# Roots of the last token group taken in one piece, and the first chunk's second layer run high weights first, in a fused attention and two-MoE kernel

## The chip, the cores and the metric

The kernel runs on one core of a Trainium2 chip. The metric is the device time of one execution in microseconds (us). TensorE is called PE here, VectorE DVE, ScalarE ACT, GpSimd POOL and SyncE, which issues most of the DMAs, SP. PE's weight loads are listed on their own as PEld.

## The reference, cut to what matters

Three layers stand one behind the other. Linear attention gives 4608 tokens of 512 values, normed by a root mean square per head of 64. A first mixture of experts routes each token to the expert with the largest logit. A second one, which this change does not touch, assigns 576 tokens to each of 8 experts.

```python
def _attn_ref(q, k, v, g_norm):
    kv = np.einsum('bhsd,bhse->bhde', k, v)
    out = np.einsum('bhsd,bhde->bhse', q, kv)
    rms = np.sqrt(np.mean(out * out, axis=-1, keepdims=True) + 1e-06)
    return (out / rms * g_norm).astype(np.float32)

def _moe_ref(x, expert_emb, tau, w1, w2):
    ...
    logits = xn @ en.T / tau
    expert_idx = np.argmax(logits, axis=1)
    ...
    for e in range(E):
        mask = expert_idx == e
        h = np.maximum(x[mask] @ w1[e], 0.0)
        out[mask] = gate_w[mask, None] * (h @ w2[e])
```

## The kernel before, in words

**Groups and steps.** The tokens come in four groups (gi 0 to 3) of nine tiles. Each group takes ten steps i. A step transposes a piece of q two steps ahead (`qa`: PE into `tp`, ACT copies to `qT`) and multiplies an earlier piece by the kv product (`qb`: PE into a bank `mm`; ACT copies the result to `xo`, squares it to `sq` and copies the logits to `lp`). DVE sums the squares of the step before to `s`. The last two steps are the short tail (`xt`).

**The group's end.** `group_end(gi)` takes roots of the sums (`rsqrt`: a square root on ACT, then four DVE operations on `yy`, `ww`, `r`), scales the logits, reduces them over the heads to `lg`, finds the expert (`mx`, `w`, `ix`, one-hot `P`) and stores the rows to `xbuf`. `slots()` then multiplies `P` by triangular and full matrices on PE (`trm`, `ones`), scans the counts (`bs`, `ue`, `run`), builds one-hots (`ohb`, `oha`) and has PE add them to a table of slots (`table`, `tabi`). It is a generator: `pump()` or `next(ge)` takes it one stage further, so its engine work lies between the steps in the order written. For the last group `part` splits the roots into columns of tiles 0 and 1, of 2 and 3, and of 4, and `LASTP` says at which steps the stages are taken.

**First expert, first chunk.** Slots of expert 0 filled by the first three groups (320 columns, tiles 0 to 2) are gathered early from `xbuf` (`xg`, and `kvx` for the third), scaled by their roots (`normed`), and transposed (`xtile`) to high and low parts `xh`, `xl` at the steps that `XT0` names. `first0` runs both expert layers on that chunk: 192 matmuls of 320 columns, three products for each weight (high weight by high and low data, low weight by high data). `stream` hands them out in portions (`PEW`, in us), between which the last group's end is emitted; `ROWS` places the transposes of the remaining tiles 3 to 5 near the end. The chunk's banks `mm` are two: a layer-1 bank is free again when DVE has written `hl` from it. Tiles 3 to 5 are gathered once the last group's `table` is done, and chunk 1 (288 columns) begins with them.

**Weights.** A piece is 128 x 1024 numbers (512 KB), loaded to one of three buffers `wraw` by SP; ACT casts it to `whi`, and DVE takes the rest to `wlo`, which frees the buffer. Pieces 0 to 3 are layer 1 of expert 0, 4 to 7 layer 2. `LSUB` holds DVE parts that are put off until after the gather.

**Aside.** `w2g_ops` is a list of small DVE products (`rc`, 128 of them) that prepare second-router weights for experts 6 and 7. `ASIDE` says how many are emitted at five places of each of the experts 1 to 5; some are left over for expert 6, which takes one after each of four layer-1 pieces, and `run_gen(wg)` takes what remains.

Of the kernel before, what the change touches and what calls it, by code (L numbers as in the profile page):

```python
# [7 lines left out]
F32 = mybir.dt.float32  # L8
# [30 lines left out]

SURE = 6  # L40

ASIDE = (1, 5, 6, 6, 3)

EARLY = 0

PEW = ((1, 2.0), (1, 4.2), (1, 2.0), (2, 3.3))

EVAC = (
# [7 lines left out]

LOADS = {19: 1, 21: 2, 23: 3, 27: 4, 30: 5, 31: 6}

LASTP = (4, 5, 6, 8, 9)

NSQ = 4

NYR = 4

XT0 = (4, 5, 5)

ROWS = (2.6, 1.3, 0.2)

# [12 lines left out]
def fused_kernel(ctx, tc, q, k, v, g_norm, emb, tau, w1, w2, wgate, v1, v2, out):  # L81
# [146 lines left out]
    def run_gen(g):  # L228
        for _ in g:
            pass  # L230
# [155 lines left out]
    def group_end(gi):  # L386
# [31 lines left out]
        def part(a, b):  # L418

            c = slice(16 * a, min(16 * b, TG * H))  # L420
            V.tensor_scalar(uu[:, c], s1[:, c], 1.0 / D, 1e-6, op0=OP.mult, op1=OP.add)
            if last:
                yield
            yield from rsqrt(r[:, c], uu[:, c], yy[:, c], ww[:, c])
            V.tensor_tensor(lp[:, c], lp[:, c], r[:, c, None].to_broadcast([128, c.stop - c.start, E]), op=OP.mult)

            f, of = lp.rearrange("p c n -> p (c n)"), lg.rearrange("p c n -> p (c n)")
            m = min(b, 4)
            if a < m:
                V.tensor_reduce(of[:, 16 * a:16 * m].rearrange("p (a x) -> p a x", a=m - a),  # L430
                                f[:, 128 * a:128 * m].rearrange("p (a h x) -> p a x h", a=m - a, h=H), axis=AX.X, op=OP.add)
            if b == 5:
                V.tensor_reduce(of[:, 64:], f[:, 512:].rearrange("p (h x) -> p x h", h=H), axis=AX.X, op=OP.add)
            for u_ in range(a, b):
                m = 2 if u_ < 4 else 1
                x = G["x", u_]
                nc.gpsimd.tensor_copy(x[:, :, HD:HD + E], lg[:, 2 * u_:2 * u_ + m])
                if u_ < 4:
                    nc.gpsimd.tensor_copy(x[:, :, HD + E:], r[:, 16 * u_:16 * u_ + 16].rearrange("p (h r) -> p r h", r=2))
                else:  # L440
                    nc.gpsimd.tensor_copy(x[:, 0, HD + E:].rearrange("p (g h s) -> p g s h", g=2, h=2),
                                          r[:, 64:72].rearrange("p (g s h) -> p g s h", g=2, s=2))

        if last:

            p0, p1, p2 = part(0, 2), part(2, 4), part(4, 5)
            next(p0)
            yield
            next(p0)
            yield  # L450
            run_gen(p0)
            yield
            next(p1)
            yield
            next(p1)
            yield
            next(p2)
            next(p2)
            run_gen(p1)
            yield  # L460
            run_gen(p2)
            for u_ in range(5):
                store(u_)
        else:
            yield from part(0, 5)
            yield
        w = t8("w")
        mx = mk(gp, [128, TG], F32, "mx", bufs=2)
# [94 lines left out]
    def wload(upto, q=nc.sync):  # L563
        while WS["load"] < min(upto, len(WQ)):
            key, t, off, pat = WQ[WS["load"]]
            raw = mk(wpA, [128, 1024], F32, "wraw", bufs=3)
            q.dma_start(raw.rearrange("p (a c) -> p a c", c=pat[-1][1]), src(t, off, pat))
            RAW[key] = raw
            WS["load"] += 1
# [166 lines left out]
    def layer1(m, e, f, c):  # L736
        run_gen(layer1_g(m, e, f, c))

    def layer1_g(m, e, f, c):

        N = WID[m, e][c]
        keep = (m, e) == (0, E - 1)
        if f == 0 and not keep:
            k = SLOT[m, e][c]
            HT[m, e, c] = [mk(mp, [128, KF, COLS[k]], F32R, f"h{p}{k}") for p in "hl"]
        whi, wlo = (w.rearrange("p (a c) -> p a c", a=KD) for w in WT[m, e, 0, f])
        xh, xl = XT[m, e, c]
        ps = mk(psum, [128, 2, 512], F32, "mm")
        for t in range(2):
            o = ps[:, t, :N]  # L750
            for kd in range(KD):
                a, b = whi[:, kd, t * 128:(t + 1) * 128], wlo[:, kd, t * 128:(t + 1) * 128]
                nc.tensor.matmul(o, a, xh[:, kd, :N], start=(kd == 0), stop=False)  # L753
                nc.tensor.matmul(o, a, xl[:, kd, :N], start=False, stop=False)  # L754
                nc.tensor.matmul(o, b, xh[:, kd, :N], start=False, stop=(kd == KD - 1))  # L755
                yield 3 * N / 2400
# [20 lines left out]
    def layer2_g(e, c, dp, mid=None):  # L777

        N = WID[0, e][c]
        if dp == 0:  # L780
            k = SLOT[0, e][c]
            YT[e, c] = mk(mp, [128, KD, COLS[k]], F32, f"yT{k}")
        hh, hl = HT[0, e, c]
        apart = (e, c, dp) == (E - 1, 1, 1)
        ps = mk(psum, [128, 2, 512], F32, "mm")
        order = [(t, kf) for t in range(2) for kf in range(KF)]
        if (e, c, dp) == (0, 0, 0):
            order.sort(key=lambda x: x[1] // (KF // 2))
        for t, kf in order:
            if apart and t and kf == 0:  # L790
                ps = mk(psum, [128, 2, 512], F32, "mm")
            o = ps[:, t, :N]
            d = (2 * dp + t) * 128
            a, b = (w[:, d:d + 128] for w in wb(0, e, kf))
            nc.tensor.matmul(o, a, hh[:, kf, :N], start=(kf == 0), stop=False)  # L795
            nc.tensor.matmul(o, a, hl[:, kf, :N], start=False, stop=False)  # L796
            nc.tensor.matmul(o, b, hh[:, kf, :N], start=False, stop=(kf == KF - 1))  # L797
            yield 3 * N / 2400
            if kf == KF - 1:
                if mid and t == 0:  # L800
                    mid()
# [199 lines left out]
    for n, st in enumerate(steps):  # L1001
# [26 lines left out]
        if gi == NG - 1:  # L1028
            if i == 0:
                kvs.close()  # L1030
                wpB = ctx.enter_context(tc.tile_pool(name="wpB", bufs=RING // 2))
                mo0 = ExitStack()
                MP["xh1"] = MP["xl1"] = mo0.enter_context(tc.tile_pool(name="moex", bufs=1))
                WP.append(wpB)
            elif n in CASTS:
                wcast(1, V, 1)
            if i == EARLY:
                index(0, 3)
                gather(0, 0, 0, 3, early=True)
            if i == LASTP[0]:  # L1040
                ge = group_end(gi)
            if i in LASTP:
                next(ge)
        if gi == 0 and i < 4:
            pump()
    late()
# [3 lines left out]


    LSUB = []

    def late_cast(f):
        if WS["cast"] < RING:
            wcast(2 if f > 2 else 1, later=LSUB if f in (1, 2) else None)

    def first0():
        for f in range(4):
            yield from layer1_g(0, 0, f, 0)  # L1060
            late_cast(f)
        yield from layer2_g(0, 0, 0)
        yield from layer2_g(0, 0, 1)

    f0 = first0()
    pe = stream(f0)
    for i, (m, us) in enumerate(PEW):
        for _ in range(m):
            next(ge)
        if i:  # L1070
            pump()
        pe(us)
    run_gen(ge)
    while bg:
# [3 lines left out]
    while LSUB:  # L1078
        LSUB.pop(0)(V)
    pe(1.1)  # L1080
    done = sum(us for _, us in PEW) + 1.1
    total = 64 * CUT * 3 / 2400
    for i, us in enumerate(ROWS):
        pe(total - us - done)
# [436 lines left out]
    for f in range(4):  # L1521
        layer1(0, e6, f, 0)
        if f == 0:
            gt = gates(e6)
        next(gt, None)
        if f == 0:
            ro = rows_out(e6 - 1, 1)
            next(ro)
            next(ro)
        if f == 1:  # L1530
            run_gen(ro)
        wcast()
        aside(1)
        if f == 1:
            gather(0, e7)
    norm()
# [742 lines left out]
```

## Time and profile before

| | us |
|---|---|
| median of three runs | 1047.08 |
| lowest and highest run | 1041.48, 1047.2 |
| profiled execution, its time | 1044.7 |
| profiled execution, its span | 1042.8 |
| PE busy in the span | 1005.1 (96%) |
| DVE busy | 731.3 (70%) |
| ACT busy | 527.8 (51%) |

The rows that follow the change come from the profiled execution. Their times run from the start of its span.

### The profile page before, as it was taken

The numbers are of one execution on the slowest core, as the hardware profiler recorded it, in microseconds if no ns is written. First come the engines' busy times: TensorE is split into PE (matmuls) and PEld (weight loads), VectorE is DVE, ScalarE is ACT, GpSimd is POOL, SyncE is SP. The second block draws the span as 40 slices with busy tenths as digits, with TensorE's granted clock in tenths as the row PEclk, the third lists the DMA queues.
The fourth block names the chain that finished last, engine by engine and source line by source line (L and its number), as shares of the span: only waits on it lengthen the run. The fifth ranks groups of instructions, "written<-read, shape, count | busy, mean of one in ns | idle before, by whom it ended". The sixth has DMA issues, their size and how long they took to land. (4 is left out here: it accounts for less than half of the span.)

```text
span 1042.8 us, 20500 instructions
## 1 busy us (share of the span) xinstructions
PE 1005.1 (96%) x8177; PEld 924.3 (89%) x8177; DVE 731.3 (70%) x1526; ACT 527.8 (51%) x915; POOL 178.8 (17%) x310
## 2 busy tenths in 40 slices
PE   8888889999999999999899999999999999999998
PEld 7777789999999999999888988898989898989896
DVE  4367876558877868786866874869595958686760
ACT  2567636665445354444432323656565555556551
POOL 2000231101010201011000113131313132322211
PEclk8999899999999999999999999999999999999999
DMA  9999655554434343432301115343434342425211
GB/s 287 373 344 342 221 191 184 173 159 133 153 105 151 115 144 116 131 131 99 126 21 64 39 59 196 128 156 121 145 110 153 101 153 101 161 102 164 101 47 46
DMA packets 94679, 152.46 MB, mean 146 GB/s; under 512 B 11321, under 2 KB 52281, under 8 KB 94579
## 3 DMA queue, kind: packets, MB, share of 16 engines
q1 hardware_dynamic: 85539, 122.18, 35.1%
q0 software_dynamic: 9040, 28.93, 8.6%
q8 instruction: 65, 1.06, 0.4%
q14 instruction: 35, 0.29, 0.1%
HBM read 121.26 MB, written 29.82 MB: 145 GB/s over the span
## 5 line engine op out<-in xcount | busy, mean ns | idle before, releaser
L753 PE MATMUL mm<-xh,whi 128*128 128x256 f32 (+7 forms) x512 | 154.6, 302 | 5.1 <-DVE hl L762 4.1
L795 PE MATMUL mm<-hh,whi 128*128 128x256 f32 (+7 forms) x512 | 155.5, 304 | 0.3 <-ACT whi L583 0.3
L797 PE MATMUL mm<-hh,wlo 128*128 128x256 f32 (+7 forms) x512 | 151.6, 296 | 0.7 <-DVE wlo L589 0.7
L754 PE MATMUL mm<-xl,whi 128*128 128x256 f32 (+7 forms) x512 | 151.7, 296 | 0.3 <-DVE xl L714 0.3
L755 PE MATMUL mm<-xh,wlo 128*128 128x256 f32 (+7 forms) x512 | 151.9, 297 | 0.0
L796 PE MATMUL mm<-hl,whi 128*128 128x256 f32 (+7 forms) x512 | 151.5, 296 | 0.0
L589 DVE TENSOR_TENSOR wlo<-wraw,whi 128x1024 fp32r<-128x1024 f32 x72 | 87.7, 1222 | 34.9 <-ACT whi L583 34.7
L753 PEld LDWEIGHTS mm<-xh,whi 128*128 128x128 f32 x512 | 96.9, 189 | 7.4 <-DVE hl L762 5.5
L795 PEld LDWEIGHTS mm<-hh,whi 128*128 128x128 f32 x512 | 96.6, 189 | 2.2 <-ACT whi L583 0.6
L797 PEld LDWEIGHTS mm<-hh,wlo 128*128 128x128 f32 x512 | 96.2, 188 | 1.5 <-DVE wlo L589 1.5
L754 PEld LDWEIGHTS mm<-xl,whi 128*128 128x128 f32 x512 | 96.8, 189 | 0.5 <-DVE xl L714 0.5
L755 PEld LDWEIGHTS mm<-xh,wlo 128*128 128x128 f32 x512 | 96.8, 189 | 0.0
L796 PEld LDWEIGHTS mm<-hl,whi 128*128 128x128 f32 x512 | 96.6, 189 | 0.0
L906 DVE SCALAR_TENSOR_TENSOR rc<-xg,big 128x512 bf16<-128x512 f32 x128 | 88.1, 688 | 8.8 <-ACT big L898 5.8
L807 ACT COPY yT<-mm 128x512 f32<-128x512 f32 (+7 forms) x31 | 19.9, 642 | 140.7 <-PE mm L797 140.7
L583 ACT CAST whi<-wraw 128x1024 fp32r<-128x1024 f32 x72 | 74.9, 1043 | 2.6 <-DMA wraw<-in_moe_w 2.5
L688 POOL DMA_INDIRECT xg<-xbuf,tabi x40 | 41.3, 1033 | 201.8 <-ACT sj L635 88.5
L761 ACT ACTIVATE hh<-mm 128x512 fp32r<-128x512 f32 (+7 forms) x56 | 36.9, 659 | 72.5 <-PE mm L755 72.0
L1942 DVE TENSOR_TENSOR wlo<-wraw,whi 128x1024 fp32r<-128x1024 f32 (+1 forms) x63 | 61.0, 987 | 11.6 <-ACT whi L1945 11.6
L2199 POOL DMA_INDIRECT out<-tm,ti x38 | 41.4, 1091 | 145.5 <-ACT tm L2197 126.1
L762 DVE SCALAR_TENSOR_TENSOR hl<-mm,hh 128x512 fp32r<-128x512 f32 (+7 forms) x56 | 42.7, 762 | 30.0 <-ACT hh L761 29.5
L2184 PE MATMUL mA<-whi,hx 128*128 128x512 f32 x136 | 56.9, 418 | 0.0
(393 smaller groups left out, 2571.3 us busy)
## 6 DMA issues: line engine op xcount, KB each, us to landing
wraw<-in_moe_w SPq DMA_DIRECT2D x128, 512.0 KB
kmain<-in_k SPq DMA_DIRECT2D x16, 576.0 KB
vmain<-in_v SPq DMA_DIRECT2D x16, 576.0 KB
xbuf<-xo SPq DMA_DIRECT2D x16, 528.0 KB
qmain<-in_q SPq DMA_DIRECT2D x16, 512.0 KB
ybuf<-yr SPq DMA_DIRECT2D x29, 260.0 KB
xg<-in_moe_w SPq DMA_DIRECT2D x16, 256.0 KB
xg<-in_moe_w_gate SPq DMA_DIRECT2D x8, 256.0 KB
```

The costliest lines, as they stand in the source:

```text
L583: nc.scalar.copy(hi, raw)
L589: eng.tensor_tensor(lo, raw, hi.bitcast(F32), op=OP.subtract)
L753: nc.tensor.matmul(o, a, xh[:, kd, :N], start=(kd == 0), stop=False)
L754: nc.tensor.matmul(o, a, xl[:, kd, :N], start=False, stop=False)
L755: nc.tensor.matmul(o, b, xh[:, kd, :N], start=False, stop=(kd == KD - 1))
L762: V.scalar_tensor_tensor(hl, ps[:, :, :N], 0.0, hh.bitcast(F32), op0=OP.max, op1=OP.subtract)
L795: nc.tensor.matmul(o, a, hh[:, kf, :N], start=(kf == 0), stop=False)
L796: nc.tensor.matmul(o, a, hl[:, kf, :N], start=False, stop=False)
L797: nc.tensor.matmul(o, b, hh[:, kf, :N], start=False, stop=(kf == KF - 1))
L906: V.scalar_tensor_tensor(junk, raws[i], 1.0, wgB[:, x], op0=OP.mult, op1=OP.mult, accum_out=w2g[:, i // KF, i % KF, x:x + 1])
L1942: V.tensor_tensor(l, x, h.bitcast(F32), op=OP.subtract)
L2184: nc.tensor.matmul(ps[:, x_, :], hh, a, start=(kf == 0), stop=False)
```

## The change

The roots of the last group are taken in one part, as in the other groups, and its stages are all emitted inside the stream of the first chunk (`LASTP` is gone; `PEW` is now five portions). The transposes of the early tiles go one step later (`XT0`). In the first chunk, the last piece of layer 1 runs its high-weight products first and its low-weight ones last, and layer 2 of the chunk is a new function that holds two banks and runs the high weights of kf 0 to 5 of both halves, then those of kf 6 and 7, then all low weights. DVE's parts for pieces 4 to 7 are all put off until after the gather. Piece 6 is loaded not to a `wraw` buffer but to the memory in which the chunk's result `yT1` will lie. `ASIDE` grows by two products for each expert, and expert 6 takes none one by one.

```diff
-ASIDE = (1, 5, 6, 6, 3)
+ASIDE = (1, 6, 6, 6, 4)
-PEW = ((1, 2.0), (1, 4.2), (1, 2.0), (2, 3.3))
+PEW = (3.3, 6.2, 0.0, 0.4, 5.3)
-LASTP = (4, 5, 6, 8, 9)
-XT0 = (4, 5, 5)
+XT0 = (5, 6, 6)
...
+        yield from part(0, 5)
         if last:
-            p0, p1, p2 = part(0, 2), part(2, 4), part(4, 5)
...
-            raw = mk(wpA, [128, 1024], F32, "wraw", bufs=3)
+            if WS["load"] == RING - 2:
+                raw = mk(mp, [128, KD, COLS[1]], F32, "yT1").rearrange("p a b -> p (a b)")[:, :1024]
+            else:
+                raw = mk(wpA, [128, 1024], F32, "wraw", bufs=3)
...
+        both = [(t, kd) for t in range(2) for kd in range(KD)]
+        for part in ((1, 2) if apart else (3,)):
+            for t, kd in both:
...
+    def layer2_apart():
+        ...
+        ps = [mk(psum, [128, 2, 512], F32, "mm") for dp in range(2)]
+        most = range(KF - 2)
+        order = [(dp, t, kf, 0) for dp in range(2) for t in range(2) for kf in most]
+        order += [(dp, t, kf, 0) for dp in range(2) for t in range(2) for kf in range(KF - 2, KF)]
+        order += [(dp, t, kf, 1) for dp in range(2) for t in range(2) for kf in range(KF)]
...
-            if i == LASTP[0]:
-                ge = group_end(gi)
-            if i in LASTP:
-                next(ge)
...
+    wload(RING - 1)
     def first0():
         for f in range(4):
-            yield from layer1_g(0, 0, f, 0)
-            late_cast(f)
-        yield from layer2_g(0, 0, 0)
-        yield from layer2_g(0, 0, 1)
+            yield from layer1_g(0, 0, f, 0, f == 3)
+            wcast(2 if f > 2 else 1, later=LSUB, ahead=3 if f else 4)
+        yield from layer2_apart()
...
+    ge = group_end(NG - 1)
+    next(ge)
+    for i, us in enumerate(PEW):
+        next(ge)
         if i:
             pump()
+        if i == 2:
+            LSUB.pop(0)(V)
         pe(us)
...
         wcast()
-        aside(1)
         if f == 1:
             gather(0, e7)
```

PE's order in steps 4 to 6 of the last group: `tp<-qmain` and `qtail` are `qa`, `mm<-kvx,qT` is `qb`, `sm<-ident,xg` and `kvx` are the early tiles. Before:

```order
L355 MATMUL mm<-kvx_177,qT 128x144 x4
L710 MATMUL sm<-ident,xg_1822 128x128 x4
L496 LDWEIGHTS trm
L496 MATMUL sm<-P,trm 128x72
...
L338 MATMUL tp<-ident,qmain 128x128 x4
L355 MATMUL mm<-kvx_177,qT 128x144 x4
L710 MATMUL sm<-ident,xg_1824 128x128 x4
L710 MATMUL sm<-ident,kvx_174 128x64 x4
L338 MATMUL tp<-ident,qtail 128x128 x2
```

Now:

```order
L353 MATMUL mm<-kvx_177,qT 128x144 x4
L477 LDWEIGHTS trm
L477 MATMUL sm<-P,trm 128x72
...
L336 MATMUL tp<-ident,qmain 128x128 x4
L353 MATMUL mm<-kvx_177,qT 128x144 x4
L694 MATMUL sm<-ident,xg_1822 128x128 x4
L336 MATMUL tp<-ident,qtail 128x128 x2
L353 MATMUL mm<-kvx_177,qT 128x144 x4
L694 MATMUL sm<-ident,xg_1824 128x128 x4
L694 MATMUL sm<-ident,kvx_174 128x64 x4
```

The first early tile moved behind the slot matmuls of group 2 and one whole step; the other two moved behind one more `qb`.

DVE's order where the last sums of squares end and the last group's expert is found (`s` sums, `uu` to `lg` the roots and logits, `mx` to `P` the expert). Before:

```order
L380 TENSOR_REDUCE s_1781<-sq 128x4 x2
L421 TENSOR_SCALAR uu<-s_1781 128x8
L236 RECIPROCAL yy<-ww 128x32
...
L425 TENSOR_TENSOR lp<-lp,r 128x256
L430 TENSOR_REDUCE lg<-lp 128x32
L236 RECIPROCAL yy<-ww 128x8
...
L433 TENSOR_REDUCE lg<-lp 128x8
L469 TENSOR_REDUCE mx<-lg 128x9
...
L477 TENSOR_TENSOR P<-iof,ixall 128x72
```

Now:

```order
L378 TENSOR_REDUCE s_1781<-sq 128x4 x2
L419 TENSOR_SCALAR uu<-s_1781 128x72
L234 RECIPROCAL yy<-ww 128x72
...
L421 TENSOR_TENSOR lp<-lp,r 128x576
L426 TENSOR_REDUCE lg<-lp 128x64
L429 TENSOR_REDUCE lg<-lp 128x8
L749 SCALAR_TENSOR_TENSOR hl_2086<-mm,hh_2085 128x2x320
L450 TENSOR_REDUCE mx<-lg 128x9
...
L458 TENSOR_TENSOR P<-iof,ixall 128x72
```

All root work now stands behind the last sum, once and wider, and the first `hl` of the chunk comes between the logits and the maximum.

DVE's order in expert 6, from the last `hl` of its chunk 0 to the first of its chunk 1. Before:

```order
L906 SCALAR_TENSOR_TENSOR rc,w2g<-xg_6193,big 128x512
L762 SCALAR_TENSOR_TENSOR hl_6254<-mm,hh_6253 128x2x256
...
L589 TENSOR_TENSOR wlo<-wraw,whi 128x1024
L906 SCALAR_TENSOR_TENSOR rc,w2g<-xg_6193,big 128x512
L670 TENSOR_TENSOR xg<-xg 128x512
L672 TENSOR_TENSOR xg<-xg,gB 128x512
L906 SCALAR_TENSOR_TENSOR rc,w2g<-xg_6193,big 128x512 x4
L762 SCALAR_TENSOR_TENSOR hl_6469<-mm,hh_6468 128x2x320
```

Now:

```order
L749 SCALAR_TENSOR_TENSOR hl_6247<-mm,hh_6246 128x2x256
L643 TENSOR_REDUCE gts<-gx 128x5
L644 TENSOR_SCALAR gts<-gts 128x5
L645 RECIPROCAL gts<-gts 128x5
L573 TENSOR_TENSOR wlo<-wraw,whi 128x1024
L654 TENSOR_TENSOR xg<-xg 128x512
L656 TENSOR_TENSOR xg<-xg,gB 128x512
L749 SCALAR_TENSOR_TENSOR hl_6454<-mm,hh_6453 128x2x320
```

Six `rc` products are gone from this piece, eight from expert 6 in all.

## Rows read from the trace of the kernel before

**Rows 1.** Waits of PE, 95 to 180 us: releaser, total us, times, longest.
```profile
PE sm L710 <- DVE xg L670: 3.0, 1, 3.0
...
PE sm L496 <- DVE P L477: 1.5, 1, 1.5
...
PE mm L797 <- DVE wlo L589: 0.7, 1, 0.7
...
PE mm L753 <- DVE hl L762: 0.5, 1, 0.5
PE mm L795 <- ACT whi L583: 0.3, 1, 0.3
```

**Rows 2.** Stretch, length; busy us of PE, PEld, DVE, ACT, POOL; granted clock; DMA.
```profile
113.30:124.76 11.46, 9.24 (x78) 8.20 (x78) 8.92 (x26) 7.24 (x22) 0.00 (x0) 0.70 0.50 193
124.76:161.17 36.41, 32.48 (x225) 30.26 (x225) 25.93 (x66) 12.53 (x23) 9.62 (x22) 1.00 0.61 200
...
113.40:120.10 6.70, 5.71 (x27) 5.19 (x28) 4.72 (x13) 2.95 (x8) 0.00 (x0) 0.50 0.84 323
```

**Rows 3.** Timeline of PE: start, us, instruction, [idle before <- releaser].
```profile
124.76 0.41 PE L753 MATMUL mm<-xh,whi 128*128 128x320 f32 x1 [0.16 <-ACT lp L377]
...
136.23 0.31 PE L753 MATMUL mm<-xh,whi 128*128 128x320 f32 x1
...
140.63 0.31 PE L753 MATMUL mm<-xh,whi 128*128 128x320 f32 x1
...
161.17 0.40 PE L753 MATMUL mm<-xh,whi 128*128 128x288 f32 x1 [0.67 <-ACT xh L713]
```

**Rows 4.** Timeline of DVE, group 2's roots to the last group's slots.
```profile
107.34 0.59 DVE L236 RECIPROCAL yy<-ww 128x72 f32<-128x72 f32 x1
...
112.51 0.23 DVE L477 TENSOR_TENSOR P<-iof,ixall 128x72 bf16<-128x72 f32 x1
...
120.42 1.14 DVE L714 SCALAR_TENSOR_TENSOR xl<-sm,gcol,xh 128x512 fp32r<-128x512 f32 x2 [1.97 <-ACT xh L713]
...
128.54 0.74 DVE L380 TENSOR_REDUCE s<-sq 128x4 f32<-128x256 f32 x2
...
134.00 0.23 DVE L477 TENSOR_TENSOR P<-iof,ixall 128x72 bf16<-128x72 f32 x1
...
135.11 1.22 DVE L589 TENSOR_TENSOR wlo<-wraw,whi 128x1024 fp32r<-128x1024 f32 x1
136.24 0.30 DVE L501 TENSOR_TENSOR_SCAN bs<-seg,sm 128x72 f32<-128x72 f32 x1
...
139.21 0.76 DVE L522 TENSOR_TENSOR ohb<-iob,sf 128x1152 bf16<-128x1152 bf16 x1
```

**Rows 5.** Timeline of POOL: the first gather after the last group's table.
```profile
142.90 1.16 POOL L688 DMA_INDIRECT xg<-xbuf,tabi  x1 [9.55 <-DVE tabi L997]
```

**Rows 6.** Timeline of DVE: scaling of the third late tile.
```profile
152.86 0.69 DVE L670 TENSOR_TENSOR xg<-xg 96x512 f32<-96x512 f32 x1 [1.03 <-DMA xg<-xbuf,tabi]
```

**Rows 7.** Waits of PE, 490 to 660 us.
```profile
PE mm L753 <- DVE hl L762: 3.3, 2, 2.9
```

**Rows 8.** Timeline of PE in expert 6, chunk 1.
```profile
508.48 0.41 PE L753 MATMUL mm<-xh,whi 128*128 128x320 f32 x1 [2.87 <-DVE hl L762]
...
509.55 0.47 PE L753 MATMUL mm<-xh,whi 128*128 128x320 f32 x1
...
512.49 0.43 PE L755 MATMUL mm<-xh,wlo 128*128 128x320 f32 x1
```

**Rows 9.** Timeline of DVE in the same place.
```profile
504.80 0.69 DVE L906 SCALAR_TENSOR_TENSOR rc<-xg,big 128x512 bf16<-128x512 f32 x1
...
507.61 0.82 DVE L762 SCALAR_TENSOR_TENSOR hl<-mm,hh 128x640 fp32r<-128x640 f32 x1
```

**Rows 10.** Waits of PE, 180 to 500 us: the only row.
```profile
PE mm L753 <- DVE hl L762: 0.3, 1, 0.3
```

**Rows 11.** Timeline of DVE at the start of expert 3.
```profile
309.32 0.69 DVE L762 SCALAR_TENSOR_TENSOR hl<-mm,hh 128x512 fp32r<-128x512 f32 x1 [2.74 <-ACT hh L761]
```

More of the change, by code (lines that the diff above doesn't have):

```diff
@@ L421, in part @@
             V.tensor_scalar(uu[:, c], s1[:, c], 1.0 / D, 1e-6, op0=OP.mult, op1=OP.add)
-            if last:
-                yield
             yield from rsqrt(r[:, c], uu[:, c], yy[:, c], ww[:, c])
@@ L433, in part @@
                 V.tensor_reduce(of[:, 64:], f[:, 512:].rearrange("p (h x) -> p x h", h=H), axis=AX.X, op=OP.add)
+            if last:
+                yield
             for u_ in range(a, b):
@@ L442, in part @@
                                           r[:, 64:72].rearrange("p (g s h) -> p g s h", g=2, s=2))
+        yield from part(0, 5)
         if last:
-            p0, p1, p2 = part(0, 2), part(2, 4), part(4, 5)
[L447 to L461, printed above, removed]
             for u_ in range(5):
@@ L464, in group_end @@
         else:
-            yield from part(0, 5)
             yield
@@ L737, in layer1, with layer1_g @@
         run_gen(layer1_g(m, e, f, c))
-    def layer1_g(m, e, f, c):
+    def layer1_g(m, e, f, c, apart=False):
         N = WID[m, e][c]
@@ L748, in layer1_g @@
         ps = mk(psum, [128, 2, 512], F32, "mm")
-        for t in range(2):
-            o = ps[:, t, :N]
-            for kd in range(KD):
+        both = [(t, kd) for t in range(2) for kd in range(KD)]
+        for part in ((1, 2) if apart else (3,)):
+            for t, kd in both:
+                o = ps[:, t, :N]
                 a, b = whi[:, kd, t * 128:(t + 1) * 128], wlo[:, kd, t * 128:(t + 1) * 128]
[L753 to L756, printed above, removed]
+                if part & 1:
+                    nc.tensor.matmul(o, a, xh[:, kd, :N], start=(kd == 0), stop=False)
+                    nc.tensor.matmul(o, a, xl[:, kd, :N], start=False, stop=False)
+                if part & 2:
+                    nc.tensor.matmul(o, b, xh[:, kd, :N], start=False, stop=(kd == KD - 1))
+                yield {1: 2, 2: 1, 3: 3}[part] * N / 2400
         if keep:
@@ L785, in layer2_g @@
         ps = mk(psum, [128, 2, 512], F32, "mm")
[L786 to L789, printed above, removed]
+        for t, kf in [(t, kf) for t in range(2) for kf in range(KF)]:
             if apart and t and kf == 0:
@@ L807, in layer2_g @@
             nc.scalar.copy(YT[e, c][:, 2 * dp:2 * dp + 2, :N], ps[:, :, :N])
+    def layer2_apart():
+        N = WID[0, 0][0]
+        YT[0, 0] = y = mk(mp, [128, KD, COLS[SLOT[0, 0][0]]], F32, f"yT{SLOT[0, 0][0]}")
+        hh, hl = HT[0, 0, 0]
+        ps = [mk(psum, [128, 2, 512], F32, "mm") for dp in range(2)]
[3 more added lines that the diff above has]
+        order += [(dp, t, kf, 1) for dp in range(2) for t in range(2) for kf in range(KF)]
+        for dp, t, kf, low in order:
+            d = (2 * dp + t) * 128
+            o = ps[dp][:, t, :N]
+            w = wb(0, 0, kf)[low][:, d:d + 128]
+            if low:
+                nc.tensor.matmul(o, w, hh[:, kf, :N], start=False, stop=(kf == KF - 1))
+            else:
+                nc.tensor.matmul(o, w, hh[:, kf, :N], start=(kf == 0), stop=False)
+                nc.tensor.matmul(o, w, hl[:, kf, :N], start=False, stop=False)
+            yield (2 - low) * N / 2400
+            if low and t == 1 and kf == KF - 1:
+                nc.scalar.copy(y[:, 2 * dp:2 * dp + 2, :N], ps[dp][:, :, :N])
     def tiles_of(e, c):
@@ L1052, in fused_kernel @@
     LSUB = []
-    def late_cast(f):
-        if WS["cast"] < RING:
-            wcast(2 if f > 2 else 1, later=LSUB if f in (1, 2) else None)
+    wload(RING - 1)
     def first0():
         for f in range(4):
-            yield from layer1_g(0, 0, f, 0)
-            late_cast(f)
-        yield from layer2_g(0, 0, 0)
-        yield from layer2_g(0, 0, 1)
+            yield from layer1_g(0, 0, f, 0, f == 3)
+            wcast(2 if f > 2 else 1, later=LSUB, ahead=3 if f else 4)
+        yield from layer2_apart()
     f0 = first0()
     pe = stream(f0)
-    for i, (m, us) in enumerate(PEW):
-        for _ in range(m):
-            next(ge)
+    ge = group_end(NG - 1)
+    next(ge)
+    for i, us in enumerate(PEW):
+        next(ge)
         if i:
             pump()
+        if i == 2:
+            LSUB.pop(0)(V)
         pe(us)
@@ L1080, in fused_kernel @@
     pe(1.1)
-    done = sum(us for _, us in PEW) + 1.1
+    done = sum(PEW) + 1.1
     total = 64 * CUT * 3 / 2400
```

## The prediction

> **What bounds the kernel now.** I read the waits of PE by stretch first, then the busy time and granted clock of the stretches in which PE waits, then the timelines of PE and of the engine that releases it. PE is busy 96% of the span, and from 180 to 500 us it waits for another engine once, for 0.3 us [rows 10]. So PE's own work sets the pace there, and whatever is saved ahead of 180 us should stay saved at the end. Three places are left where the edits touch a wait of PE.
>
> First, the last steps of group 3. PE waits 3.0 us for DVE to scale the early tiles [rows 1]; then the clock is granted at 0.50, the 1.2 GHz level, from 113.4 to 120.1 us, with PE busy 5.71 of 6.70 us [rows 2]. ACT, which copies and squares each step's result, is busy only 7.24 of 11.46 us in this stretch [rows 2]: it starves behind PE. Second, the first chunk of expert 0, from 124.76 to 161.17 us [rows 3], in which PE idles 3.9 us [rows 2]: 1.5 for the one-hot P of the last group, 0.5 for a bank that `hl` releases, 0.3 and 0.7 for pieces of weights that came late [rows 1], and the rest for the chunk's end. Third, expert 6 at 508 us: 3.3 us in two waits for `hl`, the longer of 2.87 us [rows 7, 8], again with slow matmuls behind it.
>
> **The change part by part.** *Early tiles one step later.* The transposes that wait for the scaled rows move behind a whole step, and DVE does the scaling behind two sums and the slot arithmetic of group 2. PE no longer stands still with a step's products undone. What it meets instead: the `trm` product, now ahead of the tiles, wants P of group 2, ready at 112.74 us [rows 4]; PE's step ends near 111.3, so some 1.4 us stay as a wait, and another of about 1 us for the first tile. Neither starves ACT for long, as it is a step behind. I carry the loss over to ACT, whose last copies free the bank of the chunk's first matmul [rows 3]. It idled 11.46 - 7.24 = 4.2 us; I keep 1.1 of them (the `run` copies that wait for DVE, and the first tile), so the first matmul comes at 121.7: **3.1 us** gained. Bounds: 4.2 if ACT never waits, 0.6 if the clock falls again (below).
>
> *Roots in one part.* One set of operations on 72 columns replaces three sets, but nothing of it can run before the last sum. Group 2 did it so: from the reciprocal to P took 112.74 - 107.34 = 5.4 us with one sum of about 0.6 inside [rows 4]; here one `hl` (0.8) stands in the sum's place, and the scaled sum and ACT's root come ahead (0.5), in all 6.1 us. Before, 134.23 - 129.28 = 5.0 us passed from the last sum to P [rows 4], so by itself the edit costs 1.1. But DVE reaches the last sum earlier: 129.28 less the 1.97 us for which it waited [rows 4], less some 2.5 of early root work that no longer lies ahead: 124.8. P then comes at 130.9, 3.3 us earlier, while PE, with 72 matmuls at (140.63 - 136.23)/30 = 0.147 us [rows 3] and a table product ahead, asks for it at 132.7. The waits for P (1.5) and for the first `hl` go; the second is close, as DVE writes this `hl` by 129.2 and PE wants the bank at 129.1, so I leave 0.3.
>
> *The slots of the last group.* After `trm` at 132.9, DVE takes from the scan to the one-hots 139.21 - 136.24 = 3.0 us with one `hl` inside, now with a `wlo` of 1.1 added [rows 4]: the third bank is released at 137.0. PE ends layer 1 at 132.9 + 24 x 0.147 = 136.4, and its second layer wants that bank: a new wait of 0.7 us. Behind it on PE stands everything to the end of the chunk. The table ends near 140.8 and the gather starts near 141.9, against 142.90 [rows 5], 1.0 us earlier.
>
> *Piece 6 into `yT1`, low weights last.* Piece 6 is loaded while the DMAs idle, piece 7 when piece 3's `wlo` ends, near 135, and the low parts are wanted only at the end. The waits of 0.3 and 0.7 [rows 1] go at no cost. On SP the load stands ahead of the last group's stores, which wait for the logits anyway. The `wlo` parts that are put off queue on DVE between the table and the scaling of the late tiles, 4 x 1.1 us, and end near 145.5, before the rows land.
>
> *The late tiles.* PE wants the third at 137.0 + 96 x 0.147 + some 1.6 of table product and transposes, near 152.6. Its rows were scaled at 152.86 with the gather 1.0 later [rows 5, 6]; 1.0 earlier and with one load of four less in the way, DVE ends it by 152.5 at the latest. This cover is thin, a few tenths, so I charge nothing but keep the price: each 0.1 us that the rows are later than that costs PE 0.1.
>
> The chunk so loses 1.5 + 0.5 + 0.3 + 0.7 = 3.0 us of waits [rows 1] and four restarts of 0.1 (a matmul after a wait lasts 0.41 for 0.31, [rows 3, 8]), and takes on 0.7 + 0.3: **2.4 us** gained. Bounds: 3.9, its whole idle time [rows 2], and -1, if new waits eat it.
>
> *Asides.* In expert 6 six `rc` products leave the stretch of DVE ahead of the `hl` for which PE waited; four of them took 507.61 - 504.80 = 2.8 us, 0.7 each [rows 9]. With 4.2 us less ahead of it, and ready data, the `hl` is done by about 504.4, before PE asks (505.3, behind its transposes). So 3.3 us [rows 7] with two restarts of 0.1, and the slow matmuls behind them: 11 of them from 509.55 to 512.49 took 2.94 us [rows 8] where 0.147 each makes 1.6, thus 1.4 with the twelfth. Together **4.9 us**. Bounds: 0, if another engine is late at the same place, and 5.1. The ten products that go to experts 1 to 5 add 1.5 us of DVE in each expert; at expert 3's start DVE idled 2.74 us [rows 11], so they cost nothing; without that cover each would cost 0.7.
>
> **Sum.** 3.1 + 2.4 + 4.9 = 10.4 us off the profiled execution's 1044.7: 1034.3. That execution lies 2.4 under the median of the three runs and 3.2 above the lowest, so I leave the number where the profile puts it: 1034.
>
> **The rivals.** *The clock falls in the short waits.* In the trace the clock fell after waits of 3.0 and 2.87 us [rows 1, 2, 8], but stayed at 1.00 through the whole chunk with its 3.9 us of idle time in pieces of at most 1.5 [rows 2]. The new order leaves about 1.4 and 1 us close together near 112 us. If the clock falls there, some 5 us of PE work run at the 1.2 GHz level and ACT again starves: 2.5 us of the first term go, 1036.8. The Trainium skill ("TensorE: Matmul & The Clock Gate", "A second HAM failure mode: psum-queue depth-cycling") holds that frequent micro-idling of PE between groups of matmuls lets the clock swing; by that rule this rival would be likely, and the chunk, which idles so at full clock, speaks against it. I give it 0.15.
>
> *The rows come late.* The new bound would be the last group's chain (P, table, gather, scaling), which moves by 1.0 us while PE moves by 5.5. If the rows land with the delays of before and DVE's queue of `wlo` holds the scaling, PE waits 2 to 3 us for the tiles near 150, and half the gains before it are gone: 1037. Against it: one load fewer competes. 0.15.
>
> *The waits in expert 6 stay in part.* If ACT's casts or an earlier `hl` hold the bank, the wait shrinks to 1 to 2 us without the slow clock: 1036.5. 0.06.
>
> *Nothing for the weights.* The load into `yT1` waits until the attention's readers of that memory are done; if that is as late as 137 us, layer 2 waits as before: 1035.5. 0.04.
>
> *Slower.* The place is DVE at the end of experts 1 to 5, four products in a row more than a layer covers. If they put the first `hl` of the next expert behind the point where PE wants its bank, PE waits as in expert 6, about 3 us with 1.4 of slow clock, five times: 22 us, 1056. It decides once the addition of 1.5 us exceeds the 2.74 us of cover [rows 11] and the two layer-1 pieces that PE has in hand. That needs more than twice the delay: 0.04.
>
> **How the numbers follow.** The forecast has 0.56, the rivals the numbers above. A difference under 1%, 10.5 us here, is about what this measurement cannot tell from none, and the forecast's 10.4 lies at that border. Its own uncertainty is some 2.5 us, more of it towards a larger gain: stalls too short for a row of their own are in the chunk's 36.41 us [rows 2] but not in my sum, and the idle time of the three places is 4.2 + 3.9 + 5.1 = 13.2 us, that is 1031.5. So I count 0.43 of its 0.56 as faster by over 1% and 0.13 as within it; of the rivals with 7 to 9 us of gain 0.03 go to faster. Faster 0.46, same 0.50, slower 0.04. The range: 1031.5 less most of the distance from the profile to the lowest run gives 1029 below; the rivals up to 1037 and the median's 2.4 above the profile, which hardly come together in full, give 1041 above. Outside lie the slower case, and small parts of the others.
>
> **What would show it.** Right: in the profile after, no wait of PE for the scaled tiles near 112 us and a granted clock of 1.00 from 110 to 160; the chunk's first matmul near 121.7 and the next chunk's first near 155.7; P before PE's `trm`; a wait of under 1 us ahead of layer 2; in expert 6 no PE wait for `hl` and no stretch under full clock. Wrong: a wait for `xg` near 150, a clock of 0.50 near 115, or a row of waits for `hl` in experts 1 to 5.

## The result, and the profile after

| | before | after |
|---|---|---|
| median, us (7 runs each) | 1046.85 | 1036.05 |
| lowest and highest run | 1041.48, 1049.28 | 1033.47, 1037.71 |
| profiled execution, span | 1042.8 | 1035.4 |

The ratio of the times is 0.9906, with a 95% interval of 0.9881 to 0.9931: 10.8 us between the medians (9.8 by the ratio), with 10.4 forecast. The time lies 2 us from the prediction and inside its range.

The waits of PE in the changed kernel, 95 to 180 us (releaser, total us, times, longest), against [rows 1]:

```profile
PE sm L477 <- DVE P L458: 1.3, 1, 1.3
...
PE sm L694 <- DVE xg L654: 0.8, 1, 0.8
PE mm L810 <- DVE hl L749: 0.7, 1, 0.7
...
PE mm L739 <- ACT xh L697: 0.5, 1, 0.5
...
PE tp L694 <- DVE xl L698: 0.2, 1, 0.2
```

The wait of 3.0 for the scaled tile has become two, of 1.3 for P of group 2 and 0.8 for the tile. The chunk's waits for P, for its first `hl` and for weights are gone. New are 0.7 ahead of layer 2 (L810), as forecast, and 0.2 ahead of the last late tile, for which nothing was charged.

Busy time and clock of the stretches (the columns of [rows 2]): the last steps up to the chunk's first matmul, the chunk, and the end of the experts. The profile after ran 3.42 us later ahead of all edits (a in the table below), so the 113.30 of [rows 2] is 116.72 here:

```profile
116.72:124.97 8.25, 6.30 (x75) 5.33 (x73) 8.04 (x24) 7.12 (x21) 0.00 (x0) 1.00 0.66 244
124.97:157.92 32.95, 31.49 (x224) 30.09 (x225) 24.30 (x56) 12.36 (x22) 9.62 (x21) 1.00 0.51 179
480.00:520.00 40.00, 40.00 (x345) 36.80 (x344) 26.55 (x53) 23.28 (x38) 0.69 (x5) 1.00 0.37 124
```

The clock is 1.00 in all three. The last steps take 8.25 us for 11.46; ACT's work in them is the same (7.12 us for 7.24), and its idle time is down from 4.2 to 1.1 us. The chunk takes 32.95 us for 36.41. In expert 6, where PE waited 3.3 us [rows 7], it is now busy without a gap.

The timelines of PE, and of DVE in the last group's chain, where [rows 3, 4] stood:

```profile
136.17 0.29 PE L477 MATMUL sm<-P,trm 128*128 128x72 bf16 x1
...
140.86 0.39 PE L810 MATMUL mm<-hh,whi 128*128 128x320 f32 x1 [0.75 <-DVE hl L749]
...
156.70 0.55 PE L694 MATMUL tp<-ident,xg 96*128 96x96 f32 x4 [0.21 <-DVE xl L698]
```
```profile
133.49 0.23 DVE L458 TENSOR_TENSOR P<-iof,ixall 128x72 bf16<-128x72 f32 x1
...
136.63 0.30 DVE L482 TENSOR_TENSOR_SCAN bs<-seg,sm 128x72 f32<-128x72 f32 x1 [1.95 <-PE sm L478]
...
144.40 0.24 DVE L521 TENSOR_TENSOR table<-table,sm 128x80 f32<-128x80 f32 x1 [1.40 <-PE sm L517]
```

P is there 2.4 us before PE's `trm`, and now DVE waits for PE: 1.95 us at the scan and 1.40 at the table. The chain from P to the gather is held by PE's portions (PEW), no longer by DVE. The gather starts at 145.70 (POOL):

```profile
145.70 1.16 POOL L672 DMA_INDIRECT xg<-xbuf,tabi  x1 [12.60 <-DVE tabi L1004]
```

Last, PE's waits from 180 to 500 us, the place of the slower rival: 

```profile
PE mm L739 <- DVE hl L749: 0.2, 1, 0.2
```

One row, as before [rows 10]: the products that moved to experts 1 to 5 cost nothing. They are eight, not the ten of the prediction: `ASIDE` offers ten more places, but all 128 products are done by 480 us, before expert 6, where the kernel before ran eight.

**One table for all kernels.** The experiments are read by four landmarks of each profiled execution, in us: the start of ACT's last copy to `kvx` (a), which lies ahead of every edit; the first matmul of the first chunk (b); that of the next chunk (c); the first product of the second router's logits in expert 6 (d). "Rounds" is the time from the first to the last matmul of the second router's rounds behind d. The ratio is the time against the kernel before, with its interval.

| kernel | a | a to b | b to c | c to d | rounds | ratio |
|---|---|---|---|---|---|---|
| before | 102.27 | 22.49 | 36.41 | 359.33 | 60.6 | 1 |
| after | 105.69 | 19.28 | 32.95 | 353.71 | 61.9 | 0.9906 [0.9881, 0.9931] |
| after_again | 103.94 | 19.29 | 33.10 | 353.91 | 60.6 | 0.9906 [0.9878, 0.9933] |
| asides_undone | 105.55 | 19.90 | 33.18 | 359.54 | 60.7 | 0.9955 [0.9934, 0.9977] |
| early_undone | 106.73 | 21.11 | 32.91 | 353.81 | 62.0 | 0.9944 [0.9919, 0.9968] |
| chunk_alone | 103.91 | 21.23 | 33.36 | 360.65 | 60.6 | 0.9984 [0.9970, 0.9998] |
| early_alone | 105.97 | 19.37 | 38.33 | 359.26 | 60.6 | 0.9996 [0.9979, 1.0012] |
| asides_alone | 108.91 | 21.08 | 37.00 | 353.65 | 60.6 | 0.9951 [0.9930, 0.9973] |
| roots_in_parts | 104.37 | 19.37 | 36.62 | 354.09 | 60.6 | 0.9923 [0.9897, 0.9948] |
| piece6_in_wraw | 106.70 | 19.98 | 40.10 | 353.77 | 61.8 | 0.9960 [0.9940, 0.9979] |
| low_by_half | 106.02 | 19.27 | 35.18 | 353.74 | 60.6 | 0.9933 [0.9906, 0.9960] |
| portions | 105.89 | 19.28 | 32.05 | 353.85 | 61.9 | 0.9894 [0.9866, 0.9922] |
| best1 | 106.41 | 19.39 | 33.22 | 354.04 | 60.6 | 0.9900 [0.9875, 0.9924] |

Between before and after the three middle stretches give 3.2 + 3.5 + 5.6 = 12.3 us. The spans differ by 7.4, as a came 3.4 us later and the rounds took 1.3 longer, neither by the change (the last section).

### The profile page after: what moved, and what is told of

Same layout as the page of the kernel before. It is cut to its first block, busy times and chain, and to the rows that moved or that the text cites. A ratio compares the mean times of both kernels' runs of the same rounds, so it can differ in the third digit from the quotient of the medians.

```text
span 1035.4 us, 20479 instructions
## 1 busy us (share of the span) xinstructions
PE 999.9 (97%) x8177; PEld 920.5 (89%) x8177; DVE 729.5 (70%) x1513; ACT 528.0 (51%) x913; POOL 181.6 (18%) x310
## 5 line engine op out<-in xcount | busy, mean ns | idle before, releaser
L779 PE MATMUL mm<-hh,whi 128*128 128x256 f32 (+7 forms) x480 | 146.0, 304 | 0.0
L780 PE MATMUL mm<-hl,whi 128*128 128x256 f32 (+7 forms) x480 | 142.4, 297 | 0.0
L781 PE MATMUL mm<-hh,wlo 128*128 128x256 f32 (+7 forms) x480 | 142.1, 296 | 0.0
L779 PEld LDWEIGHTS mm<-hh,whi 128*128 128x128 f32 x480 | 91.3, 190 | 1.5 <-issue 0.5
L780 PEld LDWEIGHTS mm<-hl,whi 128*128 128x128 f32 x480 | 91.3, 190 | 0.0
L781 PEld LDWEIGHTS mm<-hh,wlo 128*128 128x128 f32 x480 | 90.8, 189 | 0.0
```

## The experiments

**asides_undone**: the changed kernel with the products back in expert 6.

```diff
-ASIDE = (1, 6, 6, 6, 4)
+ASIDE = (1, 5, 6, 6, 3)
...
         wcast()
+        aside(1)
         if f == 1:
             gather(0, e7)
```

> The changed kernel with the old ASIDE and the products back in expert 6. Theory (three separate gains that add up: early tiles 3.2, chunk 3.5, asides 5.6, as the two traces place them): 5.6 us slower than the changed kernel, so about 1041.7, with the wait of PE for `hl` of 2.9 us back in expert 6 and slow matmuls behind it. Rival (the wait in expert 6 was set by when PE came there, not by the products ahead of `hl` on DVE): no wait over 1 us, and at most 1.5 us slower.

Measured: 0.9955 for 0.9906, that is 0.0049 of 1045 or 5.1 us lost, give or take 3.4 by the two intervals; c to d is 359.54. The wait is back to the tenth (PE, 470 to 660 us):

```profile
PE mm L739 <- DVE hl L749: 3.3, 2, 2.9
```

The products ahead of `hl` set that wait, not the time at which PE came.

**asides_alone**: the kernel before with the new ASIDE and without `aside(1)`, the reverse of the edit above.

> The kernel before with the new ASIDE and no products in expert 6, all else as before. Theory (the gain in expert 6 does not rest on the other edits, and the fall of the clock near 557 us in the second router's rounds, seen in both kernels that have the new asides so far, comes with them): the first product of the second router's logits comes 5.7 us earlier against the chunk's end, the rounds take 62 us for 60.6, and the whole gains 4.3 us. Rival (the fall near 557 belongs to the chunk's edits or to chance): rounds of 60.6 us and 5.6 us gained.

Measured: 0.9951, or 5.1 us gained (2.8 to 7.3 by the interval); c to d is 353.65, 5.7 us less. So the asides' gain rests on no other edit. The rounds took 60.6 us, so my theory on the clock at 557 us fell, and the rival had the two stretches right.

The chunk in this profile takes 37.00 us for 36.41, and shows the clock at 0.50 in another place: at the chunk's start, ahead of the wait for P (0.78 here). PE had waited 0.68 and 0.88 us for ACT in the last step, 1.4 us apart:

```profile
127.99 0.48 PE L361 MATMUL mm<-kvx,qT 64*64 64x72 f32 x16 [0.68 <-ACT lp L377]
129.35 0.48 PE L361 MATMUL mm<-kvx,qT 64*64 64x72 f32 x16 [0.88 <-ACT lp L377]
```
```profile
132.00:134.00 2.00, 2.00 (x10) 2.00 (x8) 1.97 (x6) 0.00 (x0) 0.74 (x4) 0.50 0.32 127
```

**early_undone**: the changed kernel with the early tiles where they were.

```diff
-XT0 = (5, 6, 6)
+XT0 = (4, 5, 5)
```

> The changed kernel with XT0 = (4, 5, 5). Theory: 3.2 us slower, about 1039.3; PE waits 3 us for the scaled tile, the granted clock falls to 0.50 ahead of the chunk, and the chunk's first matmul comes some 3 us later against the start of the last group's copies. Rival (the end of the chunk is set by the rows of the late tiles, so that a later start only takes their slack): the chunk itself is shorter by 1.5 us or more, and the whole loses under 1.5 us.

Measured: 0.9944, 4.0 us lost, give or take 3.7 by the two intervals. In the trace a to b grows by 1.8 us, less than 3.2, and the chunk is unchanged (32.91), so the rival fails. PE waits for the scaled tile again, and the clock falls behind it, here in the stretch 121 to 123 us:

```profile
PE sm L694 <- DVE xg L654: 2.5, 1, 2.5
```
```profile
121.00:123.00 2.00, 2.00 (x12) 1.54 (x10) 1.19 (x5) 2.00 (x6) 0.00 (x0) 0.50 0.98 339
```

**early_alone**: the kernel before with XT0 = (5, 6, 6) and nothing else.

> The kernel before with XT0 = (5, 6, 6) alone. Theory: the chunk starts 3.2 us earlier with the clock at 1.00, and 3 us of it stay: about 1043.8. Rival (P of the last group then comes as late as before, since in the kernel before its roots are spread over the steps and DVE gets behind): the wait for P grows by 1.5 us or more, and under 1.5 us stay.

Measured: 0.9996, no gain that shows (at most 2.2 us by the interval), though a to b is 3.1 us shorter. The chunk takes 38.33 us for 36.41. The theory is wrong on the whole, and the rival is right on the place but not on the means: the wait for P did not grow (1.47 in the kernel before). What grew is the wait for group 2's one-hots ahead of it, 0.68 us for the 0.20 of before, and behind both waits the clock falls (timeline, a stretch of two us, then the chunk):

```profile
128.93 0.48 PE L536 MATMUL sm<-oha,ohb 128*128 128x80 bf16 x9 [0.68 <-DVE oha L530]
...
135.30 0.29 PE L496 MATMUL sm<-P,trm 128*128 128x72 bf16 x1 [1.41 <-DVE P L477]
```
```profile
137.00:139.00 2.00, 2.00 (x9) 2.00 (x9) 1.93 (x8) 0.00 (x0) 0.00 (x0) 0.50 0.37 105
...
125.34:163.67 38.33, 34.02 (x225) 31.77 (x225) 26.37 (x68) 12.54 (x23) 9.38 (x22) 0.96 0.59 195
```

The same place in the kernel before:

```profile
127.87 0.48 PE L536 MATMUL sm<-oha,ohb 128*128 128x80 bf16 x9 [0.20 <-DVE oha L530]
```

Of the 1.9 us more, 0.4 are idle time (38.33 - 34.02 for 36.41 - 32.48) and 1.5 are slower work.

**chunk_alone**: the changed kernel with the edits of `ASIDE` (and `aside(1)`) and of `XT0` undone, so that only the last group's end and the first chunk differ from the kernel before.

> Only the chunk stage changed: XT0 and the asides as before. Theory: 3.5 us faster than the kernel before (about 1043.3); from the chunk's first matmul to the next chunk's 33.0 us where the kernel before takes 36.4. Rival (the chunk's gain rests on the earlier start, since P and table come no earlier by themselves): 35 us or more there, and under 1.5 us of gain.

Measured: 0.9984, 1.7 us gained, between 0.2 and 3.1. The chunk takes 33.36 us, so it does not need the earlier start, as the theory has it; of its 3.05 us less time part is lost again in c to d (360.65, 1.3 more than before). That is the clock in expert 6: behind the same wait of 2.87 us PE works for 6 us at 0.50, which loses 3.0, where four us of the kernel before at 0.57 lose 1.7. The two stretches, here and then in the kernel before:

```profile
506.00:512.00 6.00, 6.00 (x22) 6.00 (x23) 4.82 (x6) 0.00 (x0) 0.00 (x0) 0.50 0.30 93
```
```profile
509.00:513.00 4.00, 4.00 (x19) 4.00 (x18) 3.97 (x6) 0.00 (x0) 0.00 (x0) 0.57 0.43 135
```

**roots_in_parts**: the changed kernel with the roots of the last group in three parts. The code of `part`, `p0` to `p2` and LASTP is the removed code of the change's diff; the portions are

```diff
-PEW = (3.3, 6.2, 0.0, 0.4, 5.3)
+LASTP = (4, 5, 6, 8, 9)
+PEW = ((1, 2.0), (1, 4.2), (1, 2.0), (2, 5.0))
```

> The changed kernel with the last group's roots in three parts again, spread over the steps and the first portions of the chunk as in the kernel before (its LASTP, and PEW = ((1, 2.0), (1, 4.2), (1, 2.0), (2, 5.0))); the early tiles, the weights and the asides stay as changed. Theory (the roots in one part are what lets the gain of the early tiles stay: spread out, they put P 9.9 us behind the chunk's first matmul, as in the run with XT0 alone): PE waits 1.4 us for P, the granted clock falls behind it as in that run, the chunk takes 34.5 to 36 us for 33.0, and the whole is 1.5 to 3 us slower than the changed kernel. Rival (the chunk's gain is the weights' alone): 33.5 us or less for the chunk and no loss over 0.5 us.

Measured: 0.9923 beside 0.9906 of after_again; their medians are 1038.01 and 1035.30, 2.7 us apart. The intervals overlap, so the times leave it open; the trace shows a chunk of 36.62 us, a little more than I expected, with the one-hots, P and the bank behind it late as in early_alone, and then a slow clock (timeline, two us, the chunk):

```profile
127.33 0.48 PE L536 MATMUL sm<-oha,ohb 128*128 128x80 bf16 x9 [0.68 <-DVE oha L530]
...
133.75 0.29 PE L496 MATMUL sm<-P,trm 128*128 128x72 bf16 x1 [1.47 <-DVE P L477]
...
134.70 0.41 PE L758 MATMUL mm<-xh,whi 128*128 128x320 f32 x1 [0.54 <-DVE hl L768]
```
```profile
137.00:139.00 2.00, 2.00 (x9) 2.00 (x8) 1.79 (x9) 0.00 (x0) 0.00 (x0) 0.50 0.82 249
...
123.74:160.36 36.62, 33.30 (x225) 31.77 (x225) 26.31 (x68) 12.41 (x23) 10.87 (x22) 0.95 0.50 168
```

early_alone and this kernel both have the new XT0 and the old roots, with the same three waits and a slow clock; in the chunk they differ by the weights' edits and PE's last portion. From 38.33 to 36.62 the idle time falls by 1.0 us, the 0.3 and 0.7 of weights that came late, and the busy time by 0.7. From 36.62 to the 32.95 of the changed kernel the roots in one part take another 1.9 of idle and 1.8 of busy time. So both shorten the chunk, by 1.7 and 3.7 us, in one execution of each. No run has the roots in one part with the weights as before.

**piece6_in_wraw**: the changed kernel without the place in `yT1`.

```diff
-            if WS["load"] == RING - 2:
-                raw = mk(mp, [128, KD, COLS[1]], F32, "yT1").rearrange("p a b -> p (a b)")[:, :1024]
-            else:
-                raw = mk(wpA, [128, 1024], F32, "wraw", bufs=3)
+            raw = mk(wpA, [128, 1024], F32, "wraw", bufs=3)
...
-    wload(RING - 1)
...
-            wcast(2 if f > 2 else 1, later=LSUB, ahead=3 if f else 4)
+            wcast(2 if f > 2 else 1, later=LSUB, ahead=3)
```

> The changed kernel with piece 6 in a `wraw` buffer again and its load where the other pieces have theirs, all else as changed. Theory (without the place in `yT1` the loads of pieces 6 and 7 wait for `wlo` parts that free buffers, the second of them behind the table): PE waits 1.5 to 3 us for `whi` of kf 6 and 7 in layer 2, near 148 us, and the whole is 1.5 to 3 us slower than the changed kernel. Rival (kf 6 and 7 come late enough in the new order without it): no wait over 0.3 us and no loss.

Measured: 0.9960, 5.6 us lost, twice what I expected. PE waits 4.1 us for two `whi`, and the clock falls behind both:

```profile
145.43 0.45 PE L807 MATMUL mm<-hh,whi 128*128 128x320 f32 x1 [1.44 <-ACT whi L564]
...
156.13 0.64 PE L807 MATMUL mm<-hh,whi 128*128 128x320 f32 x1 [2.63 <-ACT whi L564]
```
```profile
147.00:149.00 2.00, 2.00 (x13) 1.80 (x13) 0.00 (x0) 0.00 (x0) 0.00 (x0) 0.50 0.00 0
...
157.00:159.00 2.00, 2.00 (x10) 2.00 (x9) 2.00 (x4) 0.99 (x3) 0.00 (x0) 0.50 1.10 390
```

The first buffer comes free with piece 3's `wlo`, at 140.3, too late for piece 6. With the other `wlo` put off, the next comes free only behind the table, which itself waits for PE, so without the fourth place the new order costs more in the chunk (40.10 us) than the old one.

**low_by_half**: the changed kernel, with the second layer's low weights taken after each half's high ones.

```diff
-        order = [(dp, t, kf, 0) for dp in range(2) for t in range(2) for kf in most]
-        order += [(dp, t, kf, 0) for dp in range(2) for t in range(2) for kf in range(KF - 2, KF)]
-        order += [(dp, t, kf, 1) for dp in range(2) for t in range(2) for kf in range(KF)]
+        order = []
+        for dp in range(2):
+            order += [(dp, t, kf, 0) for t in range(2) for kf in most]
+            order += [(dp, t, kf, 0) for t in range(2) for kf in range(KF - 2, KF)]
+            order += [(dp, t, kf, 1) for t in range(2) for kf in range(KF)]
```

> The changed kernel, with layer 2 of the first chunk run as high then low weights of the first half, then high and low of the second. Theory (the `wlo` parts put off behind the table are ready at 147 to 149.4 us, and PE then asks for the first at 145.6): PE waits 1 to 2.5 us for `wlo` near 146 us, the chunk takes 34 to 35.5 us for 33.0, and the whole is 1 to 2.5 us slower. Rival (the wait takes the slack ahead of the late tiles' rows): PE's wait for `wlo` appears but the one before the late tiles and the bank shrinks with it, and the loss is under 0.5 us.

Measured: 0.9933, 2.8 us lost, which the intervals (some 3.9 us together) do not tell from none; in the trace the chunk takes 35.18 us, 2.2 more, as the theory has it in place and size:

```profile
PE mm L810 <- DVE wlo L573: 1.7, 3, 0.6
```

**portions**: the changed kernel with PE's second portion 2 us shorter, to take away the two waits of DVE that the profile after shows.

```diff
-PEW = (3.3, 6.2, 0.0, 0.4, 5.3)
+PEW = (3.3, 4.2, 0.0, 0.4, 5.3)
```

> The changed kernel with PEW = (3.3, 4.2, 0.0, 0.4, 5.3), so that `trm` and the table's product come 2.2 us earlier in PE's order. Theory (DVE's waits of 1.95 us for `trm` and 1.40 us for the table are PE's portions, no work): P is ready just as PE asks, the scan comes 1.9 us earlier, the third bank is free before layer 2, the gather starts near 143.4 for 145.7, and the chunk loses the wait of 0.7 and the 0.2 before the late tiles: 0.7 to 1 us faster than the changed kernel. Rival (P is late in most executions): a wait for P of 0.5 to 1 us takes the place, no gain or 0.5 slower.

Measured: 0.9894; the chunk takes 32.05 us, 0.9 less than after and 1.05 less than after_again. The wait for the last group's P did not come, that of layer 2 is down from 0.75 to 0.26, the one ahead of the last late tile is gone, and the gather starts 2.6 us earlier than the 145.70 of after (POOL, below PE):

```profile
134.18 0.29 PE L477 MATMUL sm<-P,trm 128*128 128x72 bf16 x1
...
140.57 0.41 PE L810 MATMUL mm<-hh,whi 128*128 128x320 f32 x1 [0.26 <-DVE hl L749]
```
```profile
143.12 1.16 POOL L672 DMA_INDIRECT xg<-xbuf,tabi  x1 [9.72 <-DMA wraw<-in_moe_w]
```

The trace shows the 0.9; the times (0.9894 and 0.9906, each within 0.003) cannot.

**best1**: `portions`, with the slot products of group 2 one stage later.

```diff
-            for i in range(0 if last else WAITS[0]):
+            for i in range(0 if last else WAITS[0] + (gi == NG - 2)):
```

> The changed kernel with PEW = (3.3, 4.2, 0.0, 0.4, 5.3) and the slot products of group 2 one stage later (WAITS[0] plus one for that group), so that PE does not wait for its P between the last steps. Theory: the wait of 1.2 us for P near 112 us goes, ACT starves less, and the stretch from the last copy to `kvx` to the chunk's first matmul shrinks from 19.3 to 18.3 to 19.0 us; 0.3 to 1 us faster than the kernel with the new portions alone (ratio 0.9894). Rival (ACT's own work, 18.1 us of the 19.3, and the later slots that push the end of group 2 on DVE behind the last sums set the stretch): 19.3 us or more and no gain.

Measured: 0.9900, and 19.39 us from a to b: no gain, as the rival has it. The wait for group 2's P is gone and the next one has grown from 0.8 (PE, 106 to 126 us), and the chunk gets a new wait of 1.1 for an early `hl`:

```profile
PE sm L694 <- DVE xg L654: 1.6, 1, 1.6
```

**after_again**: the changed kernel a second time.

> The changed kernel itself once more, to compare with the other kernels of this call on the same chip. Theory (the fall of the clock near 557 us is chance, as it was there in four of the nine kernels and in none of the runs that took the asides alone): the rounds take 60.6 or 61.9 us, and the ratio to the kernel before comes out between 0.988 and 0.993 again. Rival (the first 0.9906 was a lucky draw; the parts' sum is nearer to 0.993): a ratio of 0.993 or more.

Measured: 0.9906 again, and the rounds took 60.6 us, so the clock's fall at 557 us does not come in every execution of the kernel.

## Why the prediction was right, step by step

**Early tiles, 3.1 forecast.** The profile after gives 3.2, and by the mechanism named: ACT's idle time in the last steps fell from 4.2 to 1.1 us, the 1.1 that the prediction kept. The waits of 1.3 and 0.8 stand where 1.4 and 1 were put, and the clock held. But the size rests on the one execution of before. Over all profiles, a to b is 22.49, 21.11, 21.23 and 21.08 us with the old XT0 (mean 21.5) and 19.27 to 19.98 with the new (nine of them, mean 19.5): 2.0 us is what the edit brings on average. In the profile of before a came earliest of all, and the wait for the scaled tile was the longest, 3.0 us against 1.9 to 2.6 in the other three. Where the roots are taken does not move this stretch: 19.37 with the old roots (early_alone, roots_in_parts).

**Chunk stage, 2.4 forecast.** It gave 3.5, and 3.3 in after_again. By the steps: P came 8.75 us behind the chunk's first matmul (133.49 + 0.23 - 124.97; forecast 130.9 - 121.7 = 9.2), `trm` 11.2 behind it (forecast 11.0), and layer 2 waited 0.75 (forecast 0.7). The term was too small by 1.1. The idle time fell from 3.9 to 32.95 - 31.49 = 1.5 us, by 2.5, of which the sum held 3.0 - 0.7 - 0.3 = 2.0: nothing waited for the second bank, for which it charged 0.3. PE's busy time fell by another 1.0, of which the sum held 0.4 as restarts. The rest I did not trace to rows. The step on the gather was late by 0.5 (20.7 us behind the first matmul, forecast 20.2). The sum put the scan behind PE's `trm`, so DVE's wait of 1.95 us is in it; that the table then waits 1.40 us for PE's next portion is not. Hence the 0.2 ahead of the last late tile, the thin cover that the prediction kept a price for; `portions` takes it away.

The prediction worked its terms with all edits in place: its P comes earlier in part because DVE no longer waits 1.97 us for ACT. That each would bring its gain alone was only in the later expectations, and there it failed in the trace: early_alone shortens its own stretch by 3.1 and loses 1.9 of it in the chunk. By the times, early_alone gains 0.4, chunk_alone 1.7 and both together (asides_undone) 4.7; the 2.6 between that and the sum is less than the three intervals leave open, some 3 us. In early_alone and in roots_in_parts the chunk keeps the waits of the old roots and the clock falls behind them. In all profiles with the roots in one part the chunk has no wait for P, and it ran at 1.00, but for piece6_in_wraw with its waits for weights. The roots in one part so did more there than remove 1.5 + 0.5 of waits. That the loss of early_alone lies in the clock is shown for one execution; that it is so in most of them is my reading, and asides_alone shows that with the old roots the clock can fall in the chunk ahead of those waits too.

**Piece 6 and low weights last, "at no cost".** True as the two stand together: no wait of PE for weights is left in the chunk, and between early_alone and roots_in_parts the idle time falls by the 1.0 us at which the prediction valued them. They are also what the new order needs. Without the place in `yT1` the chunk takes 7.1 us more; with the low weights taken half by half, 2.2 more.

**Asides, 4.9 forecast.** c to d fell by 5.6 in the profile, and the times give 5.1 both ways (undone in the new kernel, and alone in the old one). The wait left with the products and came back with them, and the eight products in experts 1 to 5 cost nothing. The term was 0.7 too small, 0.3 of it by the clock: it lost 1.7 us in the kernel before (chunk_alone, second stretch) where the sum put 1.4. The rest has no row. The size depends on the execution, as the 3.0 lost in chunk_alone shows.

**What was luck.** The sum came out at 10.4 for a measured 10.8 in part because its errors cancel: the early tiles were sized on one execution, 1.1 above their average of 2.0, while the chunk came out 1.1 and the asides 0.7 too small.

**The rivals.** *The clock in the short waits* did not decide in the changed kernel: 1.00 from 110 to 160 us, with idle pieces of 1.34 and 0.77 us some 2.6 us apart. But as a mechanism it is real here. The Trainium skill's rule on it ("TensorE: Matmul & The Clock Gate", "A second HAM failure mode: psum-queue depth-cycling") that frequent short idling can let the clock swing agrees with early_alone and roots_in_parts, where waits under 1.5 us were followed by 0.50, and with asides_alone (0.68 and 0.88); it does not with low_by_half, which had three waits of 0.6 between pairs of matmuls at 1.00. *The rows come late* showed as 0.2 us. *The waits in expert 6 stay in part*, *nothing for the weights* and the slower case did not occur.

## What to carry to other kernels

Look, for a wait that is to be removed, at what stands next in the same chain: a stretch that begins earlier can lose that again if its own results still come late, as early_alone did. Size a gain on several executions where the wait depends on when transfers ahead of it landed. And once a chain is faster, read who waits now: here it was DVE for PE's written-out portions, and moving them is one number.

## What the runs showed of the hardware that was not expected

The same waits do not always have the same clock behind them. Behind a wait of 2.87 us in expert 6 the clock fell to 0.50, the 1.2 GHz level, and that cost 1.7 us in the kernel before and 3.0 in chunk_alone. In the first chunk PE waited 1.47 us for P and 0.54 for the bank both in the kernel before, which stayed at 1.00 [rows 1, 2], and in roots_in_parts, which fell to 0.50. Those two differ, though, by the wait for one-hots 6.4 us earlier, 0.20 and 0.68 us, so the same waits are not shown to go two ways there. In the second router's rounds they are: the changed kernel fell below full clock in one profile and not in the other, with the same list of waits of PE ahead of it (550 to 562 us of after, then of after_again):

```profile
550.00:562.00 12.00, 11.09 (x87) 10.28 (x87) 10.20 (x24) 0.58 (x1) 1.74 (x2) 0.86 0.14 44
```
```profile
550.00:562.00 12.00, 11.08 (x100) 9.88 (x98) 10.42 (x22) 0.58 (x1) 1.75 (x2) 1.00 0.14 46
```

It costs 1.3 us (61.9 for 60.6) and came in four of the thirteen profiles. What decides it stays open.

PE's instructions ahead of a are the same in all kernels, yet a lies between 102.27 and 108.91 us. PE there waits for loads of v: 2.1 us in two waits in the profile of before, up to 105 us (and 5.1 at the same line without a releaser), and after, up to 108 us (3.9 without a releaser),

```profile
PE mm L295 <- DMA vmain<-in_v: 6.0, 6, 2.3
```

This spread of 6.6 us is of the size of that between the runs of one kernel. With the 1.3 of the rounds, it is why 12.3 us of gains in the traces show as 7.4 in the spans of one pair of profiles, all but 0.2; between the medians they were 10.8 at first and 10.25 beside after_again.
